# Attention and two MoE layers on one core: the second MoE's weight decoding, first pass on another engine

## Chip, cores, metric

One core of one Trainium2 chip runs the whole kernel in one launch. The metric is the device time of one execution in microseconds (us). The engines are PE (matrix products), DVE (vector), ACT (activations), POOL (GpSimd) and SP, which only issues DMAs here.

## What is computed

Attention with a learned bias on relative positions, then two MoE-like layers, on 4 x 576 tokens:

```python
scores = q @ k.T / sqrt(64) + bias(pos)          # 4 batches, 8 heads, 576 x 576
x  = softmax(scores) @ v                         # x: 2304 x 512
h  = x @ w_in;  s = h * softmax(h)               # first MoE, 1024 wide
x  = layernorm(s) * g_ln @ w_out                 # 2304 x 512
y  = (sigmoid(x @ w_gate) * (x @ w_val)) @ w_out2   # second MoE, 1536 wide
```

The weights of both MoEs arrive as 64-bit floats. [...]

## The kernel before

**Products.** PE multiplies 16-bit floats. Every 32-bit matrix is split in a high and a low half, and three products (high x high, high x low, low x high) take the place of one. The first MoE works tile by tile (18 tiles of 128 tokens): product with `w_in` (L789), exponential and sums (L810 to L819, on ACT and DVE), the layernorm's factor and its scaling on POOL (L822, L823), transposes on PE (L832) with the split of the result by ACT and DVE (L834, L835), product with `w_out` (L846), and the result `x2` stored to DRAM. The variance that L822 needs is L820 on DVE.

**Decoding of a weight.** `decode` (L185) works on a loaded block whose 32-bit words alternate low, high. First pass, L191: the high word, read as a 32-bit float, times 2 to the power -112, into the target `w`. Low pass, L192: the upper 16 bits of the low word, scaled, as an integer, in place. Then two bit passes on DVE: L193 shifts `w` left by 3 and ors the low part in, L195 ors the sign in. L191 and L192 run on ACT. L191 reads the high words with a step of two words and writes without a gap.

**The second MoE's weights.** 18 "pairs" of 1 MB, each 128 x 1024 elements, go through `w2_dec` (L1156): gate and value weights for three column blocks jc = 0, 1, 2 (pairs 0 to 11), then the output weights (12 to 17). After a pair's decoding ACT sums its squares (L1169). When a block of gate or value is complete, its scale is made (`w2_scale_gate`, `w2_scale_val`), and `w2_split` splits it: L720 on POOL scales 128 x 512 into `w2tmp`, ACT takes the high half (L721), POOL or, for every second piece, DVE the low half (L722). For the output weights ACT does the scaling and POOL the twelve low halves.

**Loads.** `load_pair` (L1084 and on) issues each pair as two DMAs on SP's queue. Pairs 1, 2, 5 and 6 land in buffers named `gv`, all others in two buffers named `wraw` (pair 0 in a third) that take turns, so that from pair 9 on a load starts when the pair two before has been decoded.

**Uses.** The gate and value products of the second MoE's first group of tokens, j = 0 to 11, are the matmuls of L1404 into `s_ps`, 24 to a j; four of them use one column block. The text calls j = 0 "group one", j = 4 "group five" and so on. Two banks take turns; ACT's sigmoid (L1409) and DVE's product (L1410) empty them. Then come the products with the output weights (L1436) and, for the other tokens, seven products in place of eight (L1368).

**Order.** A scheduler inside the framework orders the instructions of ACT, DVE, POOL, SP and, here, PE by its own estimate of when each could run and by priorities. Each engine then runs its own list strictly in order. So a change of one instruction can move others.

Of the kernel before, what the change touches and what calls it, by code (L numbers as in the profile page):

```python
# [13 lines left out]
ACTF = mybir.ActivationFunctionType  # L14
ALU = mybir.AluOpType
# [87 lines left out]
def attn_moe_kernel(  # L103
# [7 lines left out]
    act, dve, pool, pe, sp = nc.scalar, nc.vector, nc.gpsimd, nc.tensor, nc.sync  # L111
# [70 lines left out]
    def flat(a):  # L182
        return a.rearrange("b h s d -> (b h s d)").rearrange("(p f) -> p f", p=128)

    def decode(w, raw, engine):  # L185


        wi = w.bitcast(I32)
        hw = raw[:, :, 1].bitcast(F32)
        low = raw[:, :, 0]  # L190
        act.activation(out=w, in_=hw, func=ACTF.Copy, scale=2.0 ** -112)  # L191
        act.activation(out=low, in_=low.bitcast(U16)[:, :, 1], func=ACTF.Copy, scale=2.0 ** -13, bias=-0.4999)  # L192
        dve.scalar_tensor_tensor(out=wi, in0=wi, scalar=3, in1=low, op0=ALU.logical_shift_left, op1=ALU.bitwise_or)  # L193
        if engine is dve:
            dve.scalar_tensor_tensor(out=wi, in0=raw[:, :, 1], scalar=-0x80000000, in1=wi,  # L195
                                     op0=ALU.bitwise_and, op1=ALU.bitwise_or)
        else:
            act.activation(out=hw, in_=hw, func=ACTF.Sign)
            pool.tensor_tensor(out=w, in0=w, in1=hw, op=ALU.mult)
# [528 lines left out]
    def w1_steps():  # L728
        wst = sm0.tile([128, 2, 8], F32, name="wst")

        def dec(part, i):
            if part == 0:
                kk, n = divmod(i, 2)
                raw = load_w(wr_p, w_in, slice(128 * kk, 128 * kk + 128), slice(512 * n, 512 * n + 512))
            else:
                raw = load_w(wr_p, w_out, slice(128 * i, 128 * i + 128), slice(0, DM))
            w = wf[part][:, i]
            decode(w, raw, pool if i % 8 < W1P else dve)
            j = wd_p.tile([128, 512], F32, name="wjunk", tag="wsgn")
            act.activation(out=j, in_=w, func=ACTF.Square, scale=(gcol[:, i:i + 1] if part else 1.0),  # L740
                           accum_out=wst[:, part, i:i + 1])
# [160 lines left out]
    for n, (bb, hp) in enumerate(order):  # L902
        t0 = used[bb, hp]
        for nm, src, prep, lag in (("k", k, prep_k, 0), ("v", v, prep_v, LAG_PV)):
            if (bb, hp) == (0, 0):
                continue
            f = freed[order[n - 8]] + lag + 1 if n >= 8 else 4 * (n // 2 - 1) if n >= 4 else 0
# [171 lines left out]
    def load_pair(mat, jc, cc):  # L1079
        n = len(loads) // 2  # L1080
        if n in (1, 2, 5, 6):
            raw = ring("gv", [128, 2, 512, 2], I32)
        else:
            raw = w2r_p[n in (3, 7) or (n > 8 and n % 2)].tile([128, 2, 512, 2], I32, name="wraw", tag="wraw")  # L1084
        r0 = 256 * cc + (512 * jc if mat == 2 else 0)
        src = (w_gate, w_val, w_out2)[mat]
        cols = slice(0, DM) if mat == 2 else slice(512 * jc, 512 * jc + 512)
        for c in range(2):
            with tc.issue_after(loads[-1].ins):
                loads.append(sp.dma_start(out=raw[:, c].rearrange("p f t -> p (f t)"),  # L1090
                                          in_=src[r0 + 128 * c:r0 + 128 * c + 128, cols].bitcast(I32)))
        return raw
# [63 lines left out]
    def w2_dec(mat, jc, cc):  # L1156
        raw = w2raw.pop((mat, jc, cc), None)
        if raw is None:
            raw = load_pair(mat, jc, cc)
        w = w2f[mat][:, 4 * jc + 2 * cc:4 * jc + 2 * cc + 2].rearrange("p c f -> p (c f)")  # L1160
        decode(w, raw.rearrange("p c f t -> p (c f) t"), dve)
        if mat == 1:
            j = w2d_p.tile([128, 1024], BF16, name="w2sq", tag=f"w2sq{cc}")
            for c in range(2):
                w2h["sq", jc, 2 * cc + c] = j[:, 512 * c:512 * c + 512]
        else:
            j = w2t_p.tile([128, 1024], BF16, name="w2junk", tag="w2sgn")
        n = 6 * mat + 2 * jc + cc
        act.activation(out=j, in_=w, func=ACTF.Square, accum_out=w2st[:, n:n + 1])  # L1169
# [36 lines left out]
    def decs(m, jc):  # L1206
        return [(2, lambda cc=cc: w2_dec(m, jc, cc)) for cc in range(2)]
# [40 lines left out]
    first = [sum(sizes[:g]) for g in range(len(sizes))]  # L1248
# [307 lines left out]
```

## Time and profile before

| | |
|---|---|
| median of 3 runs | 1041.68 us (1038.64 to 1043.49) |
| the profiled execution | 1044.08 us, of which the span of its instructions 1042.3 us |
| PE busy | 898.6 us, 86% of the span |
| DVE busy | 725.1 us, 70% |
| ACT busy | 644.3 us, 62% |
| POOL busy | 390.4 us, 37% |

Attention fills the time up to about 550 us. Between 550 and 670 us three things overlap: the last four tiles of the first MoE, the decoding and splitting of all weights of the second, and its first gate products. After that PE works alone for the most part. All the passes that the change touches lie between 556 and 656 us. A share of busy time over the whole span tells little here; the stage must be read by itself, and in it which wait of PE ends last.

### The profile page before, as it was taken

Reading aid. Unit: us, or ns where it says so; the run is one execution under the profiler, and the core shown is the slowest. Engines: PE = TensorE matmul, PEld = TensorE weight load, DVE = VectorE, ACT = ScalarE, POOL = GpSimd, SP = SyncE. Lnnn points to the kernel's source line nnn. Section 1 sums busy time; section 2 is a strip of 40 time slices with the busy share of each in tenths; the row PEclk is TensorE's granted clock in tenths of the full one; section 3 lists DMA queues with packets and bytes.
Section 4 is the critical chain, followed back from the end, with each engine's and each line's share of the span. In section 5 each row is a group of like instructions: output and inputs, shape, how many; then the busy total and the mean of one; then the engine's idle time right before and its main releaser. Section 6 shows DMA issues by size and latency. Waiting matters only on the chain. (4 is left out here: it accounts for less than half of the span.)

```text
span 1042.3 us, 23926 instructions
## 1 busy us (share of the span) xinstructions
PE 898.6 (86%) x9620; PEld 634.8 (61%) x9620; DVE 725.1 (70%) x1487; ACT 644.3 (62%) x1275; POOL 390.4 (37%) x362
## 2 busy tenths in 40 slices
PE   2646665679888789999998989899999999999998
PEld 2634444455666556677775656346668847866873
DVE  6878899776577676667666987659936744771760
ACT  3788886757776888878876888674333322332320
POOL 3257656565666656655650486340000000000000
PEclk9666675769998999999998999899999999999999
DMA  7988999999999899899878444101020010000001
GB/s 222 282 255 205 247 254 246 219 206 189 189 191 198 174 207 179 176 219 207 160 137 310 172 158 171 58 1 61 22 61 1 1 61 21 1 11 31 2 1 41
DMA packets 257360, 144.57 MB, mean 139 GB/s; under 512 B 216417, under 2 KB 231777, under 8 KB 257249
## 3 DMA queue, kind: packets, MB, share of 16 engines
q1 hardware_dynamic: 253952, 139.90, 56.5%
q0 software_dynamic: 2048, 1.58, 0.6%
q8 instruction: 75, 1.23, 0.5%
q10 hardware_dynamic: 1248, 1.57, 0.4%
q14 instruction: 37, 0.30, 0.1%
HBM read 80.36 MB, written 20.19 MB: 96 GB/s over the span
## 5 line engine op out<-in xcount | busy, mean ns | idle before, releaser
L616 POOL TENSOR_TENSOR p<-p,p 128x1024 f16<-128x1024 f32 x72 | 158.0, 2194 | 123.3 <-ACT p L615 86.0
L1292 DVE TENSOR_TENSOR fr<-prod,fr 128x512 f32<-128x512 f32 x126 | 85.1, 688 | 92.3 <-PE prod L1368 90.6
L1436 PE MATMUL ops<-w2f,gv 128*128 128x512 f16 x648 | 142.5, 379 | 0.0
L604 ACT ACTIVATE p<-p,m,sc 128x576 f32<-128x576 f32 x144 | 123.9, 862 | 2.4
L597 DVE CUSTOM_DVE_ANT_0 p<-score,gk 128x576 f32<-128x576 f32 x144 | 102.9, 751 | 11.6 <-PE score L579 7.0
L846 PE MATMUL x2ps<-lt,w1f 128*128 128x128 f16 x1728 | 106.2, 221 | 3.5 <-ACT lt L834 1.9
L1436 PEld LDWEIGHTS <-gv 128*128 128x128 f16 x648 | 63.4, 98 | 73.7
L1404 PE MATMUL s_ps<-xb,w2f 128*128 128x512 f16 (+1 forms) x576 | 101.4, 335 | 3.7 <-DVE acc L162 3.4
L846 PEld LDWEIGHTS <-w1f 128*128 128x128 f16 x1728 | 101.0, 99 | 4.1 <-issue 1.6
L640 PE MATMUL xps<-gk,pt 128*128 128x64 f16 (+1 forms) x2240 | 86.8, 202 | 15.8 <-DMA pt<-p 14.1
L640 PEld LDWEIGHTS <-pt 128*128 128x128 f16 (+1 forms) x2240 | 81.9, 107 | 26.3 <-DMA pt<-p 17.0
L463 PEld LDWEIGHTS <-mask 128*128 128x128 f16 (+1 forms) x1312 | 62.2, 118 | 53.3 <-issue 23.4
L1368 PEld LDWEIGHTS <-w2f 128*128 128x128 f16 x864 | 84.5, 98 | 11.8 <-issue 1.1
L1404 PEld LDWEIGHTS <-w2f 128*128 128x128 f16 x576 | 56.9, 100 | 47.0 <-issue 7.4
L1273 ACT ACTIVATE gv<-fr 128x512 f16<-128x512 f32 (+1 forms) x60 | 34.8, 586 | 81.4 <-DVE fr L1426 70.5
L789 PE MATMUL hps<-w1f,xt 128*128 128x512 f16 x312 | 78.5, 398 | 5.5 <-DVE gk L262 2.6
L463 PE MATMUL bp<-rhs,mask 128*128 128x64 f16 (+1 forms) x960 | 50.0, 220 | 28.6 <-DVE gb L489 11.5
L574 PE MATMUL score<-gk,qt 64*128 64x512 f16 x384 | 59.8, 418 | 15.4 <-DVE m L597 7.0
L1368 PEld LDWEIGHTS <-w2s 128*128 128x128 f16 x648 | 63.4, 98 | 7.3
L789 PEld LDWEIGHTS <-xt 128*128 128x128 f16 x384 | 38.1, 102 | 48.8 <-issue 14.0
L615 ACT ACTIVATE p<-p 128x1152 f16<-128x1152 f32 x54 | 62.4, 1157 | 7.0 <-DMA pt<-p 4.9
L602 ACT ACTIVATE m<-m,sc 128x1 f32<-128x1 f32 x144 | 39.3, 286 | 32.9 <-DVE m L597 32.6
(207 smaller groups left out, 1760.7 us busy)
## 6 DMA issues: line engine op xcount, KB each, us to landing
gk<-bias_d SPq DMA_DIRECT2D x24, 576.0 KB
wraw<-in_moe_w_out_dram SPq DMA_DIRECT2D x20, 512.0 KB
sraw<-in_q_dram SPq DMA_DIRECT2D x12, 384.0 KB
sraw<-in_k_dram SPq DMA_DIRECT2D x12, 384.0 KB
sraw<-in_v_dram SPq DMA_DIRECT2D x12, 384.0 KB
bias_d<-gk SPq DMA_DIRECT2D x8, 576.0 KB
qraw<-in_q_dram SPq DMA_DIRECT2D x64, 64.0 KB
kv<-in_k_dram SPq DMA_DIRECT2D x32, 128.0 KB
```

The source lines that it names most:

```text
L463: pe.matmul(big[0:np_, jj // 8, o:o + 64], lhsT, rhs[i].rearrange("p c h g -> p (c h g)"), start=(i == 0), stop=(i == 1),)
L597: dve.tensor_tensor_reduce(out=pp[:, hh], in0=score[:, 960 * hh:960 * hh + S], in1=bi, scale=1.0, scalar=-3.0e38, op0=ALU.add, op1=ALU.max ...
L604: act.activation(out=pp[:, hh], in_=pp[:, hh], func=ACTF.Exp, bias=m[:, 2 + hh:3 + hh], scale=col(C), accum_out=sm[:, c + hh:c + hh + 1])
L615: act.activation(out=hi, in_=pp, func=ACTF.Copy)
L616: pool.tensor_tensor(out=p16[:, :, 640:1152], in0=view(pp, 0, [[640, 2], [1, 512]]), in1=view(p16, 0, [[1280, 2], [1, 512]]), op=ALU.subtract)
L640: pe.matmul(o, a, b_, start=(n == 0), stop=(n == len(seq) - 1))
L789: pe.matmul(h, xt[:, xl, kk, off:off + 128], win16[:, 2 * kk + n, wl], start=(kk == 0 and xl == 0 and wl == 0), stop=(kk == 3 and xl == 1),)
L846: pe.matmul(ps[:, dc], wout16[:, f, wl, 128 * dc:128 * dc + 128], lt[:, ll, f], start=(n == 0), stop=(n == 23))
L1292: dve.tensor_tensor(out=out_, in0=a, in1=b, op=op)
L1368: pe.matmul(p[:, jf, 0:nn], w(wl, kk, jf), x(xl, kk), start=(m == 0), stop=(m == 5))
L1404: pe.matmul(ps[:, 0:n], w[:, 4 * (j // 4) + c, wl, o:o + 128], xx[:, 0:n, c, xl, :], start=(m == 0), stop=(m == 11))
L1436: pe.matmul(ps, gvs[j // 4][:, gl, j % 4, 128 * tt:128 * tt + 128], w2h16[2][:, j, wl], start=(m == 0), stop=(m == 35))
```

## The change

The second MoE's `decode` gets POOL as the engine of its first pass. The first MoE's 16 blocks keep ACT.

```diff
--- before.py
+++ after.py
@@ -182,13 +182,16 @@
     def flat(a):
         return a.rearrange("b h s d -> (b h s d)").rearrange("(p f) -> p f", p=128)
 
-    def decode(w, raw, engine):
+    def decode(w, raw, engine, first=None):
 
 
         wi = w.bitcast(I32)
         hw = raw[:, :, 1].bitcast(F32)
         low = raw[:, :, 0]
-        act.activation(out=w, in_=hw, func=ACTF.Copy, scale=2.0 ** -112)
+        if first is None:
+            act.activation(out=w, in_=hw, func=ACTF.Copy, scale=2.0 ** -112)
+        else:
+            first.tensor_scalar(out=w, in0=hw, scalar1=2.0 ** -112, scalar2=None, op0=ALU.mult)
         act.activation(out=low, in_=low.bitcast(U16)[:, :, 1], func=ACTF.Copy, scale=2.0 ** -13, bias=-0.4999)
         dve.scalar_tensor_tensor(out=wi, in0=wi, scalar=3, in1=low, op0=ALU.logical_shift_left, op1=ALU.bitwise_or)
         if engine is dve:
@@ -1158,7 +1161,7 @@
         if raw is None:
             raw = load_pair(mat, jc, cc)
         w = w2f[mat][:, 4 * jc + 2 * cc:4 * jc + 2 * cc + 2].rearrange("p c f -> p (c f)")
-        decode(w, raw.rearrange("p c f t -> p (c f) t"), dve)
+        decode(w, raw.rearrange("p c f t -> p (c f) t"), dve, pool)
         if mat == 1:
             j = w2d_p.tile([128, 1024], BF16, name="w2sq", tag=f"w2sq{cc}")
             for c in range(2):
```

Three lines are added ahead, so L192 becomes L195, L193 becomes L196, L195 becomes L198, and every line behind them moves by three; the first pass on POOL is L194.

The scheduler orders the stage anew on every engine. In names below, `wraw_9413` is pair 0, `gv_9709` pair 1, `wraw_10694`, `wraw_10703` and `wraw_10712` are pairs 15, 16 and 17; `w2f0`, `w2f1`, `w2f2` are gate, value and output weights.

DVE at the start of the stage, before. `hs_9646` is the copy of tile 14's first product:

```order
L193 SCALAR_TENSOR_TENSOR w2f0_9694<-w2f0_9694,wraw_9413 128x1024
L707 TENSOR_TENSOR xt_8631<-xtp_9623,xt_8631 128x256
L195 SCALAR_TENSOR_TENSOR w2f0_9694<-wraw_9413,w2f0_9694 128x1024
L707 TENSOR_TENSOR xt_8632<-xtp_9623,xt_8632 128x256
L800 ISA hs_9646,mm_9645<-hps_9632,zero_79 128x512
L800 ISA mm_9645 128x1
L193 SCALAR_TENSOR_TENSOR w2f0_9694<-w2f0_9694,gv_9709 128x1024
L835 TENSOR_TENSOR lt_9759<-ltp_9760,lt_9759 128x512
L800 ISA hs_9646,mm_9645<-hps_9648,zero_79 128x512
```

DVE there now:

```order
L710 TENSOR_TENSOR xt_8632<-xtp_9623,xt_8632 128x256
L803 ISA hs_9646,mm_9645<-hps_9632,zero_79 128x512
L803 ISA mm_9645 128x1
L196 SCALAR_TENSOR_TENSOR w2f0_9694<-w2f0_9694,wraw_9413 128x1024
L838 TENSOR_TENSOR lt_9759<-ltp_9760,lt_9759 128x512
L198 SCALAR_TENSOR_TENSOR w2f0_9694<-wraw_9413,w2f0_9694 128x1024
L803 ISA hs_9646,mm_9645<-hps_9648,zero_79 128x512
L803 ISA mm_9645 128x1
L196 SCALAR_TENSOR_TENSOR w2f0_9694<-w2f0_9694,gv_9709 128x1024
```

The copy of tile 14's first half product stood behind pair 0's two bit passes and now stands ahead of both.

POOL late in the stage, before, from the third value split of block 1 (`w2tmp_10342`) on:

```order
L720 TENSOR_SCALAR w2tmp_10342<-w2f1_9695,sw_81 128x512
L722 TENSOR_TENSOR w2f1_9695<-w2tmp_10342,w2f1_9695 128x512
L720 TENSOR_SCALAR w2tmp_10346<-w2f1_9695,sw_81 128x512
L720 TENSOR_SCALAR w2tmp_10553<-w2f0_9694,sw_81 128x512
L720 TENSOR_SCALAR w2tmp_10557<-w2f0_9694,sw_81 128x512
L722 TENSOR_TENSOR w2f0_9694<-w2tmp_10553,w2f0_9694 128x512
L720 TENSOR_SCALAR w2tmp_10561<-w2f0_9694,sw_81 128x512
L720 TENSOR_SCALAR w2tmp_10681<-w2f0_9694,sw_81 128x512
L722 TENSOR_TENSOR w2f0_9694<-w2tmp_10561,w2f0_9694 128x512
```

POOL there now, from pair 15's first pass on:

```order
L194 TENSOR_SCALAR w2f2_9696<-wraw_10694 128x1024
L723 TENSOR_SCALAR w2tmp_10342<-w2f1_9695,sw_81 128x512
L723 TENSOR_SCALAR w2tmp_10346<-w2f1_9695,sw_81 128x512
L725 TENSOR_TENSOR w2f1_9695<-w2tmp_10342,w2f1_9695 128x512
L194 TENSOR_SCALAR w2f2_9696<-wraw_10703 128x1024
L723 TENSOR_SCALAR w2tmp_10553<-w2f0_9694,sw_81 128x512
L723 TENSOR_SCALAR w2tmp_10557<-w2f0_9694,sw_81 128x512
L194 TENSOR_SCALAR w2f2_9696<-wraw_10712 128x1024
L725 TENSOR_TENSOR w2f0_9694<-w2tmp_10553,w2f0_9694 128x512
L723 TENSOR_SCALAR w2tmp_10561<-w2f0_9694,sw_81 128x512
```

The same splits now have the first passes of pairs 15, 16 and 17 among them, and each of these waits for a load.

ACT late in the stage, before, from pair 17's first pass on; `fr_10996` is the sigmoid of group five:

```order
L191 ACTIVATE w2f2_9696<-wraw_10712 128x1024
L192 ACTIVATE wraw_10712<-wraw_10712 128x1024
L854 DMA x2_d_58<-x2_10677 128x1024
L1169 ACTIVATE w2junk_10710,w2st_9697<-w2f2_9696 128x1024
L1273 ACTIVATE gv_10764<-fr_10927 128x512
L1409 ACTIVATE fr_10965<-s_ps_10940,sw_81 128x512
L1169 ACTIVATE w2junk_10719,w2st_9697<-w2f2_9696 128x1024
L1409 ACTIVATE fr_10996<-s_ps_10971,sw_81 128x512
```

ACT there now, from pair 16's low pass on:

```order
L195 ACTIVATE wraw_10703<-wraw_10703 128x1024
L1172 ACTIVATE w2junk_10531,w2st_9697<-w2f2_9696 128x1024
L1172 ACTIVATE w2junk_10540,w2st_9697<-w2f2_9696 128x1024
L724 ACTIVATE w2f0_9694<-w2tmp_10553 128x512
L195 ACTIVATE wraw_10712<-wraw_10712 128x1024
L724 ACTIVATE w2f0_9694<-w2tmp_10557 128x512
L1412 ACTIVATE fr_10996<-s_ps_10971,sw_81 128x512
L1412 ACTIVATE fr_11026<-s_ps_11001,sw_81 128x512
```

The first pass is gone; the sigmoid of group five stands a few places behind pair 17's low pass, as it did, and now that low pass itself waits for the load.

## Rows read from the trace of the kernel before

**Rows 1.** Busy us (instructions) of PE, PEld, DVE, ACT, POOL; then clock, DMA.
```profile
556.00:656.50 100.50, 86.07 (x740) 56.63 (x740) 84.36 (x152) 85.16 (x126) 54.16 (x40) 0.91 0.57 199
680.00:780.00 100.00, 99.28 (x603) 58.77 (x602) 75.11 (x133) 47.00 (x85) 10.44 (x9) 1.00 0.10 34
```

**Rows 2.** Timeline of PE: start us, us, instruction [idle before, what ended it].
```profile
590.81 0.24 PE L846 MATMUL x2ps<-lt,w1f 128*128 128x128 f16 x1 [1.90 <-ACT lt L834]
593.86 3.05 PE L846 MATMUL x2ps<-lt,w1f 128*128 128x128 f16 x48
603.64 4.44 PE L789 MATMUL s_ps<-w1f,xt 128*128 128x512 f16 x12 [2.31 <-DVE mm L800]
626.53 0.38 PE L1179 MATMUL tot<-w2st,ones_sb 128*128 128x1 f32 x2 [3.01 <-ACT w2junk L1169]
656.52 1.03 PE L1404 MATMUL s_ps<-xb,w2f 128*128 128x512 f16 x2 [3.43 <-DVE acc L162]
```

**Rows 3.** Line L191 (duration ns min/median/max, first and last start); and a wait.
```profile
L191 ACT ACTIVATE w2f<-wraw x14: 1106/1138/1157, 556.2 to 656.0; 128x1024 f32<-128x1024 f32 x14
L191 ACT ACTIVATE w2f<-gv x4: 1135/1176/1182, 560.0 to 583.5; 128x1024 f32<-128x1024 f32 x4
DVE w2f L193 <- ACT wraw L192: 7.2, 8, 1.7
```

**Rows 4.** Lines of POOL, ns min/median/max; then groups in 556 to 671 us.
```profile
L823 POOL TENSOR_SCALAR e<-e,mm x18: 1189/1197/3256, 264.5 to 624.5; 128x1024 f32<-128x1024 f32 x18
L720 POOL TENSOR_SCALAR w2tmp<-w2f,sw x24: 687/854/2294, 581.3 to 668.9; 128x512 f32<-128x512 f32 x24
L199 POOL TENSOR_TENSOR w1f<-w1f,wraw x8: 1284/1298/1568, 79.1 to 150.5; 128x512 f32<-128x512 f32 x8
L720 POOL TENSOR_SCALAR w2tmp<-w2f,sw 128x512 f32<-128x512 f32 x24 | 28.3, 1185 | 22.5 <-ACT w2junk L1169 14.2 <-DVE mm L811 6.8 <-DVE w2f L722 0.8
L722 POOL TENSOR_TENSOR w2f<-w2tmp,w2f 128x512 f16<-128x512 f32 x12 | 19.8, 1648 | 8.3 <-ACT w2f L721 8.1
```

**Rows 5.** Timeline of POOL and DVE where the two meet.
```profile
580.12 1.20 POOL L823 TENSOR_SCALAR e<-e,mm 128x1024 f32<-128x1024 f32 x1
580.59 1.79 DVE L193 SCALAR_TENSOR_TENSOR w2f<-w2f,gv 128x1024 int32<-128x1024 int32 x1 [0.85 <-ACT gv L192]
588.20 1.22 DVE L195 SCALAR_TENSOR_TENSOR w2f<-gv,w2f 128x1024 int32<-128x1024 int32 x1
588.31 2.12 POOL L722 TENSOR_TENSOR w2f<-w2tmp,w2f 128x512 f16<-128x512 f32 x1 [0.75 <-ACT w2f L721]
```

**Rows 6.** Timeline of DVE at the start of the stage.
```profile
559.59 1.22 DVE L195 SCALAR_TENSOR_TENSOR w2f<-wraw,w2f 128x1024 int32<-128x1024 int32 x1
564.27 0.69 DVE L800 CUSTOM_DVE_ANT_0 hs<-hps,zero 128x512 f32<-128x512 f32 x1 [3.13 <-PE hps L789]
578.26 0.15 DVE L820 TENSOR_SCALAR mm<-mm 128x1 f32<-128x1 f32 x1
```

**Rows 7.** Timeline of POOL: scalings of the last tiles.
```profile
611.64 1.19 POOL L823 TENSOR_SCALAR e<-e,mm 128x1024 f32<-128x1024 f32 x1
624.53 3.26 POOL L823 TENSOR_SCALAR e<-e,mm 128x1024 f32<-128x1024 f32 x1
```

**Rows 8.** Timeline of DVE and ACT: ends of decoded pairs, and a load's landing.
```profile
607.60 1.21 DVE L195 SCALAR_TENSOR_TENSOR w2f<-wraw,w2f 128x1024 int32<-128x1024 int32 x1
640.66 1.46 DVE L195 SCALAR_TENSOR_TENSOR w2f<-wraw,w2f 128x1024 int32<-128x1024 int32 x1
647.92 1.21 DVE L195 SCALAR_TENSOR_TENSOR w2f<-wraw,w2f 128x1024 int32<-128x1024 int32 x1
647.03 1.15 ACT L191 ACTIVATE w2f<-wraw 128x1024 f32<-128x1024 f32 x1 [0.82 <-DMA wraw<-in_moe_w_out_dram]
```

**Rows 9.** Timeline of POOL, the last split before 672; chain, groups five to eight.
```profile
670.01 1.16 POOL L722 TENSOR_TENSOR w2f<-w2tmp,w2f 128x512 f16<-128x512 f32 x1
669.05 11.46 PE s_ps L1404 x53
```

## The prediction

> **What bounds the kernel now.** I read the busy time by stage first. From 680 us on PE is busy 99.28 of 100 us, and the page's slices show it so up to the end; in the stage before, 556 to 656.5 us, it is busy 86.07 of 100.5 us while ACT (85.16) and DVE (84.36) are nearly full and POOL has 54.16 [rows 1]. The change touches that stage alone. PE's work in it is fixed, so the end of the kernel moves by as much as PE's arrival at the gate products moves. Second view: PE's own timeline, for what ended its idle time. It waits 1.90 us at 590.81 (ACT's high half of a transposed tile), 2.31 at 603.64 (DVE's copy of a product), 3.01 at 626.53 (ACT's sum of squares) and 3.43 at 656.52, where the fifth gate group begins [rows 2]. The last is named after a later DVE step; the group really waits for a bank that ACT and DVE empty late. These four, 10.7 us, are what a relief of ACT could give back.
>
> **What is removed.** ACT loses the 18 passes of L191 (14 at 1.138 and 4 at 1.176 us, medians), 20.6 us of 85 [rows 3]. None is on PE's path by itself. What they delay is the pass on the low words behind them: DVE waited 7.2 us for it in eight places [rows 3].
>
> **What is added.** POOL gets 18 passes of 1024 elements with one input. The trace has no such pass with a step of two words. The nearest row is L823, one input, 1024 elements, two operations, step one: 1.19 us when nothing blocks it [rows 4]. From below, nothing suggests less than about 1.1. From above: L199 reads one operand with the step and takes 1.284 for 512 elements, where the plain L722 takes 1.16 [rows 4, 9], so twice that difference on top, 1.44. I take 1.2, as the row with the same operand count: 21.6 us on POOL.
>
> **The port.** DVE's 1024-element pass with two SBUF inputs takes 1.22 us alone (L195 at 588.20). POOL's L722 that began 0.11 us behind it took 2.12 in place of 1.16: it ended 1.01 us after DVE did. The other way round, DVE's L193 that began under POOL's L823 took 1.79 and ended 1.06 us after that [rows 5]. So the two exclude each other, each holding the port for about 1.05 us of its 1.2.
> [...]
> The ledger from 556 to 671: DVE has 36 bit passes (37.8 us held at 1.05), 4 of L813 (4.4) and 17 short ones of 0.55 (9.4); POOL has 24 of L720 at 0.56 (13.4; 0.687 alone), 12 of L722 at 1.02 (12.2) [rows 4], 5 of L823 (5.3) and 5 of L822 at 0.43 (2.2). That is 84.7 of 115 us. The new passes add 18 x 1.05 = 18.9, making 103.6, or 90%. It fits, with 11 us of slack where there were 30. Neither end of the pass's price (1.1 to 1.44, held for 0.15 less) breaks it: 101.8 to 107.9.
>
> **The new order, step by step.** Tile 14 to 17 are the last four tiles of the first MoE; "pair" is a load of 1 MB of weights.
> 1. Entry. DVE ran the two bit passes of pair 0, the second at 559.59, while it would have waited 3.13 us for PE's product at 564.27 [rows 6]. Now that product's copy stands ahead of them, so 2.4 us of DVE work move into a stretch in which DVE does not rest. Tile 14's variance, at 578.26 before [rows 6], comes at 580.7.
> 2. First transposed tile. PE's product of tile 14, at 593.86 [rows 2], needs DVE's low half of it. Until then POOL gets three passes more (pairs 6 to 8), 3.2 us of the port; DVE's three waits for low words there (0.85, 0.27, 0.72, within the 7.2 of [rows 3]) go. So 593.9 + 2.4 + 3.2 - 1.8 = 597.7, and at worst 600 where none of the three waits was on the way; PE stands still for it.
> 3. Tiles 15 and 16. Their two scalings now stand side by side on POOL. Tile 16's was done at 611.64 + 1.19 = 612.8 [rows 7]. DVE reaches its variance 5 to 7 us after step 2's half tile (two bit passes, one of L813 and the short ones), and two scalings of 1.2 and a blocked pass follow: 607 to 610. PE has made up step 2 and leads by 2 to 3 us; its wait of 2.31 is gone.
> 4. Tile 17. Its scaling took 3.26 us from 624.53, blocked by DVE [rows 7]; I get 624.5 to 625.5 for its end in place of 627.8. The sum-of-squares matmul that cost 3.01 us now stands after the last tile. PE ends the fourth gate group 2.7 us ahead.
> 5. Group five. The 3.43 us go if the splits that it needs are done. They were done long before; now they stand on POOL behind first passes that wait for loads. Two buffers take turns, and a load starts when DVE is through with the pair two before. Before, from pair 9 to pair 15 that took (649.1 - 608.8)/3 = 13.4 us a turn [rows 8], of which the load is 4.9 (issued when the pass at 640.66 ended, landed at 647.03 [rows 8]). Step 1 to 3 put pairs 7 and 8 some 10 us behind, and POOL's splits stay at 657 to 659: group five ends near 660 where it ended near 662.
> 6. Group seven. On ACT the sigmoid of group five stands behind pair 17's low pass. By step 5 pair 15's load lands at about 652, pair 17's a turn of 10.4 to 13.4 later: 662.4 to 665.4, and group seven starts at 666 to 668.6. Before it started at 669.05 + 5 x 0.216 = 670.1 (53 matmuls in 11.46 us [rows 9]). PE leads by 1.5 to 4.6; I take 3.
> 7. Group nine needs the last gate and value splits, done at 671.2 before [rows 9] against a need at 681.6. Now at about 679, against a need at 677 to 680: nought to 2 lost. The output weights' scale follows within PE's two groups of 10.4 us, which hide it; without them it would cost 6.
> Sum: -3 us, from -4.6 to +2. Against the profiled run's 1044.08 that is 1041.1; the median of the runs, 1041.68, lies 2.4 lower, so 1038.7, rounded to **1039**.
>
> **Rivals.**
> A. ACT was the bound and the port has room. Then the four waits of [rows 2] go without the new one of step 2, and group five runs at PE's full rate: -10.7, 1031, from 1027 to 1036. For it: ACT's 85%, and the port's 11 us of slack. Against it: DVE is as full as ACT, and POOL's queue stands in order behind loads. Chance 0.28.
> B. The port becomes the bound, with the splits as its place. L720 took 1.185 us on average with 0.687 alone, a factor of 1.72 [rows 4]. If the first passes suffer the same, they take 2.06 each and push the bit passes as far; the decode turn grows by four times 0.86 from 13.4 to about 17, three turns lie between pair 11 and pair 17, so pair 17's load comes 11 us later than in step 6 and PE has lost 8 by group seven: 1050, from 1046 to 1056. It decides from a turn of 14.5 us on. Chance 0.23.
> C. The pass does not cost what one-input passes cost, but as two-input ones do: twice L722's 1.16 for 512 elements [rows 9], 2.3 us. Then 18 more us on the port make 122 of 115, and the end moves by these 7 and most of B's 8: 1055. Against it: L823. Chance 0.07.
> That the change does nothing would need POOL to skip the pass; the new order shows 18 of them.
>
> **How the numbers follow.** My forecast (1036.5 to 1046.5) has 0.42, A 0.28, B 0.23, C 0.07. A measurement of this kernel can tell about 0.5%, 5.2 us, from no change. So faster by more: 0.28; within: 0.42; slower: 0.30, with the upper part of the forecast's own range counted as within. The range runs from 1029 (A's tail left out, 0.07) to 1052 (C and the top of B left out, 0.12).
>
> **What would show it.** Right: in the profile after, 18 POOL passes of about 1.2 to 1.6 us on average; ACT near 66 us in 556 to 656; DVE's pair 0 after 564; PE's wait before tile 14's product 6 us or more; its wait of 3.0 gone; a wait of some 4 us before group seven that ACT ends. Wrong: passes above 2 us (B, C), no wait at tile 14 (A), or PE waiting at group nine for POOL's splits by more than 3 us, which would put step 7 at fault. If the load, not the queue, sets the decode turn, the turn stays at 13.4 and the forecast holds whatever the passes cost.

## The result, and the profile after

The changed kernel takes 1055.9 us (median of 4 runs, 1050.9 to 1058.9) against 1042.6 in the same session: a ratio of 1.0121, interval 1.008 to 1.0163. It is slower, by some 12.6 us by that ratio (the two medians lie 13.3 us apart), where 1039 was forecast with a range up to 1052. The execution that the trace shows is the fastest of the four, 1050.9 us with a span of 1049.1.

Executions reach this stage up to some 3 us earlier or later whatever the kernel (554.2 to 560.4 us in the traces here), so I measure the stage from the transposes of the last attention output to the first product of the later token groups. PE's timeline (start us, us, instruction, idle before and what ended it), first before, then after:

```profile
557.68 1.12 PE L689 MATMUL xtp<-id_sb,xn 128*128 128x128 f32 x4 [3.35 <-DVE xn L676]
780.06 1.47 PE L1368 MATMUL prod<-xb,w2f 128*128 128x256 f16 x12 [0.78 <-ACT ob L1440]
```
```profile
554.24 1.12 PE L692 MATMUL xtp<-id_sb,xn 128*128 128x128 f32 x4 [3.18 <-DVE xn L679]
588.73 1.97 PE L835 MATMUL ltp<-id_sb,e 128*128 128x128 f32 x8 [4.83 <-POOL e L826]
644.80 0.28 PE L1182 MATMUL tot<-w2st,ones_sb 128*128 128x1 f32 x2
667.58 15.87 PE L1407 MATMUL s_ps<-xb,w2f 128*128 128x512 f16 x60 [6.06 <-DVE fr L1413]
710.82 4.40 PE L1407 MATMUL s_ps<-xb,w2f 128*128 128x256 f16 x24 [2.42 <-DVE fr L1413]
717.55 2.78 PE L1407 MATMUL s_ps<-xb,w2f 128*128 128x256 f16 x24 [1.91 <-DVE fr L1413]
786.84 1.47 PE L1371 MATMUL prod<-xb,w2f 128*128 128x256 f16 x12 [0.78 <-ACT ob L1443]
```

The stage grew from 222.4 to 232.6 us, and what lies behind the first product is 262.2 us in both. Read from one trace, such a length is good to some 3 us: e2_forms below, whose engines run this stage in the order of before, has 219.4. PE's waits behind those transposes tell more: they add up to 13.5 us before (15.0 in e2_forms) and 23.5 after. (Line numbers from L191 on stand three higher.) The waits are others than in [rows 2]: the one of 3.01 us before the sums of squares is gone (644.80), and new ones are for tile 14's scaling on POOL, at group seven, and at 711 and 718 us, where PE hardly rested before.

Busy us by stage, as in [rows 1]:

```profile
556.00:656.50 100.50, 89.06 (x763) 58.75 (x765) 82.44 (x138) 62.29 (x95) 90.54 (x47) 0.94 0.54 185
680.00:780.00 100.00, 95.68 (x579) 57.41 (x578) 87.07 (x147) 50.84 (x95) 20.20 (x17) 0.98 0.07 25
```

ACT fell from 85.16 to 62.29, as planned. POOL rose by 36 us in that stretch, where 21.6 were priced for all passes, and from 680 us on PE now loses 3.6 us more than before, a stretch that the prediction had called full. The pass itself, which answers [rows 3], by its line (ns min/median/max, first and last start), and its first one on POOL's timeline, behind a scaling of the same size:

```profile
L194 POOL TENSOR_SCALAR w2f<-wraw x14: 2817/2864/3945, 554.5 to 665.3; 128x1024 f32<-128x1024 f32 x14
L194 POOL TENSOR_SCALAR w2f<-gv x4: 2826/3362/3838, 557.3 to 581.5; 128x1024 f32<-128x1024 f32 x4
```
```profile
553.29 1.20 POOL L826 TENSOR_SCALAR e<-e,mm 128x1024 f32<-128x1024 f32 x1
554.46 2.84 POOL L194 TENSOR_SCALAR w2f<-wraw 128x1024 f32<-128x1024 f32 x1
```

The splits' scaling that shares POOL's queue, 0.854 us in the median in [rows 4], is now at 1.040:

```profile
L723 POOL TENSOR_SCALAR w2tmp<-w2f,sw x24: 682/1040/2183, 579.2 to 683.0; 128x512 f32<-128x512 f32 x24
```

The scaling of a tile takes 1.20 us, the pass 2.84, with no DVE operation with two SBUF inputs beside it. The 18 of them come to some 57 us where 21.6 were priced.

### The profile page after: what moved, and what is told of

Read it like the earlier page. It is cut to its first block, busy times and chain, and to the rows that moved or that the text cites. A ratio compares the mean times of both kernels' runs of the same rounds, so it can differ in the third digit from the quotient of the medians.

```text
span 1049.1 us, 23952 instructions
## 1 busy us (share of the span) xinstructions
PE 899.9 (86%) x9617; PEld 636.6 (61%) x9620; DVE 738.9 (70%) x1487; ACT 626.8 (60%) x1257; POOL 450.0 (43%) x380
## 5 line engine op out<-in xcount | busy, mean ns | idle before, releaser
L1407 PE MATMUL s_ps<-xb,w2f 128*128 128x512 f16 (+1 forms) x576 | 102.9, 337 | 12.3 <-DVE fr L1413 10.6
L792 PE MATMUL hps<-w1f,xt 128*128 128x512 f16 x312 | 76.1, 389 | 5.1 <-DVE gk L265 2.4
```

Of the source, the lines that this page charges most:

```text
L792: pe.matmul(h, xt[:, xl, kk, off:off + 128], win16[:, 2 * kk + n, wl], start=(kk == 0 and xl == 0 and wl == 0), stop=(kk == 3 and xl == 1),)
L1407: pe.matmul(ps[:, 0:n], w[:, 4 * (j // 4) + c, wl, o:o + 128], xx[:, 0:n, c, xl, :], start=(m == 0), stop=(m == 11))
```

## The experiments

Ratios are to the kernel before in the same session, with 95% intervals; 1% is 10.4 us.

### What the pass costs, and why

**e2_forms** adds eleven POOL operations, each twice, behind the last tile of the kernel before.

> The kernel before, with eleven POOL operations added twice behind its last tile, where DVE is nearly idle, on scratch data (the second and third group of weights are no longer needed there): the price of each form undisturbed. Theory 1 (one operation costs): forms with one operation take 2.8 us per 1024 elements with either step, forms with two 1.2. Theory 2 (the step of two words costs): all forms with the step take 2.8, all with step one 1.2. A mixture (only one operation together with the step, or only an immediate number in place of a column) would show as just those rows at 2.8.

Their lines (ns min/median/max). In order: one operation with a step of two words, two operations with that step, one operation with step one, two with step one, and the last two again with 512 elements and a scale by column where there are two operations:

```profile
L1495 POOL TENSOR_SCALAR w2f<-w2f x2: 2860/3016/3172, 962.9 to 982.8; 128x1024 f32<-128x1024 f32 x2
L1496 POOL TENSOR_SCALAR w2f<-w2f x2: 1397/1397/1397, 965.8 to 986.0; 128x1024 f32<-128x1024 f32 x2
L1498 POOL TENSOR_SCALAR w2f<-w2f x2: 3087/3088/3089, 969.4 to 989.7; 128x1024 f32<-128x1024 f32 x2
L1499 POOL TENSOR_SCALAR w2f<-w2f x2: 1044/1049/1054, 972.6 to 992.8; 128x1024 f32<-128x1024 f32 x2
L1502 POOL TENSOR_SCALAR w2f<-w2f x2: 1487/1488/1489, 976.2 to 996.5; 128x512 f32<-128x512 f32 x2
L1503 POOL TENSOR_SCALAR w2f<-w2f,sw x2: 692/692/693, 977.8 to 998.1; 128x512 f32<-128x512 f32 x2
```

Theory 1 holds. The form with one operation costs two to three times the form with two, at either step (3.02 against 1.40 us, and 3.09 against 1.05), as it does for 512 elements (1.49 against 0.69 us). DVE was not as idle there as the expectation has it. The 0.35 us between 1.40 and 1.05 are no price of the step: both times that operation began while DVE ran one with two SBUF inputs, and it ended 1.0 us after it, as in [rows 5]. The first time, on the timelines of DVE and POOL (the DVE row holds two operations, the second from 965.50 to 966.19):

```profile
964.90 1.28 DVE L1426 SCALAR_TENSOR_TENSOR fr<-fr 128x512 f32<-128x512 f32 x2
965.81 1.40 POOL L1496 TENSOR_SCALAR w2f<-w2f 128x1024 f32<-128x1024 f32 x1
```

In the kernel of the next run the same form with the step takes 1.10 us at least, so the step adds some 0.05 us. A scale by column together with the step took 2.04 us, also between such DVE operations; its undisturbed price is open. The kernel before has no POOL scaling of the form with one operation: all write two, and in all but the tile scaling (L823) the second does nothing.

**e1_two_ops** gives the pass that second operation.

```diff
-first.tensor_scalar(out=w, in0=hw, scalar1=2.0 ** -112, scalar2=None, op0=ALU.mult)
+first.tensor_scalar(out=w, in0=hw, scalar1=2.0 ** -112, scalar2=0.0, op0=ALU.mult, op1=ALU.add)
```

> The changed kernel, with the pass on the high words written with a second operation that does nothing (multiply, then add 0), as the scaling of the splits and the other cheap POOL rows of the trace have it; the read with a step of two words stays. In the changed kernel the pass took 2.82 us undisturbed where 1.2 was priced. Theory 1 (the form with one operation is what costs): the pass falls to 1.2 to 1.5 us undisturbed, the shared port has room again, and the kernel lands where the forecast's sum had it, 1036 to 1046. Theory 2 (the step of two words is what costs): the pass stays at 2.7 to 2.9 and the kernel at 1051 to 1059. Theory 3 (the price is not the cause; POOL's splits wait in order behind passes that wait for loads): whatever the price, 1050 to 1058.

The pass fell to 1.13 us in the median (1.10 at least), and the kernel stayed at 1055.9, 1.0134 (1.0099 to 1.0169). So theory 1 was right on the price and wrong on the time, which is that of theory 3. But the scheduler had made another order for this program on all engines, so price and order had both changed. They had to be parted: the same cheap pass costs 0.65 and 0.67% less in the two orders of the next table, so this third order is worth another 7 us.

### Price and order apart

The next four kernels carry a table of one kernel's instruction order, and chain each engine's instructions by it (shortened):

```diff
+for d_ in table:
+    at_ += d_
+    i_ = traced[at_]
+    if i_.engine in last_:
+        tc.add_manual_dep(i_, last_[i_.engine].name, NoSync)   # order of issue alone, no wait
+    last_[i_.engine] = i_
```

> The pass on POOL as in the changed kernel, with its one operation, but every engine's instructions kept in the order of the kernel before; the pass stands on POOL where it stood in that kernel's overall order on ACT. Only the engine of the pass and its price differ from the kernel before. Theory P (the pass's price is the loss: 18 times 2.8 us on a port that had 30 us of slack): 1048 to 1058. Theory O (the new order is the loss, price and port matter little): 1036 to 1044.

> The order of the kernel before on every engine, and the pass on POOL with two operations (1.33 us measured in place of 3.1). Theory P: what the forecast's sum was made for, no change or better, 1034 to 1044. Theory O: the same, 1034 to 1044, and equal to the kernel with one operation in this order.

> The order of the changed kernel on every engine, but the pass on ACT as in the kernel before, at its place in the changed kernel's overall order. Nothing is added to POOL or to the port. Theory P: the loss is gone, 1038 to 1046. Theory O: it stays, 1050 to 1058.

> The order of the changed kernel on every engine, the pass on POOL with two operations. Against the changed kernel only the price of the pass differs, 1.33 in place of 3.1 us. Theory P: most of the loss is gone, 1036 to 1046. Theory O: it stays, 1050 to 1058.

| | pass on ACT | on POOL, two operations | on POOL, one operation |
|---|---|---|---|
| order of before | 1 | 1.0069 (1.0049 to 1.0090) | 1.0178 (1.0149 to 1.0206) |
| order of the changed kernel | 1.0069 (1.0041 to 1.0098) | 1.0067 (1.0042 to 1.0093) | 1.0121 (1.0080 to 1.0163) |

Neither theory holds alone; the dearest kernel, 1062.9 us, lies above the range of both. Along the lower row the changed kernel's 12.6 us are 7.2 for the new order with the pass still on ACT, nothing for the move in its cheap form, and 5.6 for the form, of which the two intervals leave anything from nothing to 1.2%. Along the upper row the move costs 7.2 in its cheap form, against both theories, and the form 11.3 more, which is clear of noise. The shares depend on the path. The order alone is a loss, so is the move alone, and the two together lose no more than either.

### What the move costs at its cheap price

Two kernels part the move into what it takes and what it gives, both in the order of before. **e10_relief_alone** leaves the 18 passes out, **e11_load_alone** keeps them on ACT and adds 17 idle ones on POOL (edits shortened, against the kernel before).

```diff
-act.activation(out=w, in_=hw, func=ACTF.Copy, scale=2.0 ** -112)                  # e10
-dve.scalar_tensor_tensor(out=wi, in0=wi, scalar=3, in1=low, op0=ALU.logical_shift_left, ...)
+dve.scalar_tensor_tensor(out=wi, in0=raw[:, :, 1], scalar=0x3FFFFFFF, in1=low, op0=ALU.bitwise_and, ...)
```
```diff
 act.activation(out=w, in_=hw, func=ACTF.Copy, scale=2.0 ** -112)                  # e11
+pool.tensor_scalar(out=spare, in0=hw, scalar1=2.0 ** -112, scalar2=0.0, op0=ALU.mult, op1=ALU.add)
```

> The kernel before in its own order on every engine, with the 18 passes on the high words left out: DVE's first bit pass reads the high word of the raw weight itself (and masks it in place of shifting it), so the weights come out wrong, but each other instruction and each order stands as it was. It shows what relieving ACT of its 20.6 us is worth when nothing is put on POOL. If ACT was the bound (rival A): 1030 to 1036. If DVE is the bound beside it: 1037 to 1043, and the change had little to win at any price.

> The kernel before in its own order, ACT's passes kept, and beside each of 17 of them a POOL operation of the same shape (two operations, 1.33 us), whose result nobody reads: it writes a part of the last weights that is decoded later. It shows what the load on POOL and the port costs by itself; no decoding step waits for it. Port theory (each meeting of a POOL operation with a DVE operation with two SBUF inputs makes one of them longer, and DVE has no slack for it): 1048 to 1056, DVE's such operations some 8 us longer in all. Chain theory (the pass now stands behind POOL's other work, so that decoding starts later): 1040 to 1045, since nothing waits for these.

The relief gives 0.9975 (0.9959 to 0.9992), 2.6 us. The load costs 1.0102 (1.0084 to 1.0120), 10.6. Together 8.0, where the whole move in this order measured 7.2. The chain theory falls: nothing waits for these operations, and they cost as much as the pass itself.

**e17_memset_load** puts an operation in their place that only writes.

```diff
-pool.tensor_scalar(out=spare, in0=hw, scalar1=2.0 ** -112, scalar2=0.0, op0=ALU.mult, op1=ALU.add)
+pool.memset(spare, 0.0)
```

> The kernel with 17 idle POOL operations beside ACT's passes, with each of them turned into one that only writes: the same 128x1024 elements set to zero, at the same place in POOL's queue. It was 1051.5 with the operation that reads and writes (1.11 to 1.13 us each undisturbed). If it is POOL's queue that costs (splits and the last scaling stand behind these operations): 1047 to 1052, for about as long an operation. If it is the meetings with DVE, it depends on whether the writing alone takes the port: DVE's operations longer and 1047 to 1052, or not longer and 1041 to 1045.

It takes 0.95 us on POOL every time, at the same places of the queue, and the kernel 1.0018 (0.9997 to 1.0038): the loss is gone, or at most 0.4%. Groups of DVE's first bit pass in 556 to 671 us (busy us, mean ns, idle before and what ended it), of before, of e11 and of e17:

```profile
L193 DVE SCALAR_TENSOR_TENSOR w2f<-w2f,wraw 128x1024 int32<-128x1024 int32 x14 | 18.6, 1332 | 7.3 <-ACT wraw L192 7.2
```
```profile
L196 DVE SCALAR_TENSOR_TENSOR w2f<-w2f,wraw 128x1024 int32<-128x1024 int32 x14 | 21.9, 1568 | 4.7 <-ACT wraw L195 4.7
```
```profile
L196 DVE SCALAR_TENSOR_TENSOR w2f<-w2f,wraw 128x1024 int32<-128x1024 int32 x14 | 18.7, 1333 | 7.4 <-ACT wraw L195 7.3
```

With the reading load these 14 passes take 3.3 us more and the waits shrink by 2.6; with the writing one both stand as before. All 36 bit passes of DVE take 47.9 us before, 55.4 with the reading load and 48.9 with the writing one, and POOL's last five tile scalings 8.0, 10.5 and 8.0. One meeting of each kind, on the timelines of POOL and DVE, e11 and then e17:

```profile
587.49 1.67 POOL L193 TENSOR_SCALAR w2f<-wraw 128x1024 f32<-128x1024 f32 x1
588.15 2.09 DVE L198 SCALAR_TENSOR_TENSOR w2f<-gv,w2f 128x1024 int32<-128x1024 int32 x1
```
```profile
583.31 0.95 POOL L193 MEMSET w2f<- 128x1024 f32 x1
583.27 1.22 DVE L198 SCALAR_TENSOR_TENSOR w2f<-gv,w2f 128x1024 int32<-128x1024 int32 x1
```

Below, both run at once and neither is longer than alone (0.95 and 1.22 us). Above, both are: 1.67 us where the least in e11 is 1.11, and 2.09 in place of 1.22. So the price of the load is these meetings, and a longer queue on POOL by itself cost nothing that could be measured (1.0018). The traces show that the two hold each other up, not where: "the port" is the prediction's name for it. Two differences stay between e11 and e17. The operation that reads also holds the raw buffer, but each ended 2.6 us or more before DVE was through with that buffer, so the next load never waited for it. And it waits for its own load, which the one that only writes does not: in e11 POOL stood 13.8 us for loads. The chain of work that ended last in e11 has no load on it between 555 and 672 us, so these waits did not set the time there. In the changed kernel that chain has three:

```profile
603.25 7.38 DMA wraw<-in_moe_w_val_dram
619.62 5.00 DMA wraw<-in_moe_w_out_dram
644.28 5.83 DMA wraw<-in_moe_w_out_dram
```

No run parts what these cost from the price of the pass.

### What relieves the port

**e4_scale_on_act** and **e12_old_order_scale_on_act** move the scaling of the 24 gate and value splits from POOL to ACT, in the changed kernel and in the cheap form in the old order; **e13_two_ops_scale_on_act** is the cheap form with the order that it gets by itself. **e5_every_second** leaves every other pass on ACT.

```diff
-act if mat == 2 else None, dve if mat < 2 and c % 2 else None)     # e4, e12, e13: in w2_split
+act, dve if mat < 2 and c % 2 else None)
-decode(w, raw.rearrange("p c f t -> p (c f) t"), dve, pool)        # e5
+decode(w, raw.rearrange("p c f t -> p (c f) t"), dve, pool if cc else None)
```

> The changed kernel, with the scaling of the 24 gate and value splits by ACT in place of POOL. It takes 24 times 0.69 us from POOL and the port and gives ACT some 24 times 0.65, which brings ACT back from 62 to about 78 of the 100.5 us. If the full port is what the change lost its time to (99% of 556 to 671 us in the changed kernel), this gives back 13 us of port: 1043 to 1049. If instead the passes' place in POOL's queue is what costs, the low halves of the splits still stand behind them: 1049 to 1056.

> The changed kernel, with only the second pass of each two on POOL (nine of 18), the others on ACT as before. Price and port theory: 9 passes of 2.7 us put 24 us on the port beside the 84.7 of the kernel before, 109 of 115: it just fits, and ACT is 10 us lighter: 1038 to 1045. Queue theory: half the passes still stand ahead of the splits and wait for their loads: about half the loss, 1046 to 1050.

> The order of the kernel before, the pass on POOL with two operations, and the scaling of the 24 gate and value splits moved from POOL to ACT, at its place in the overall order. POOL loses 24 times 0.69 us and gains 18 times 1.33. Port theory: the meetings fall back, DVE's operations are at most some 4 us longer than before, and of the 8 us that the pass cost in this order most are gone: 1041 to 1047. Otherwise, with ACT again near 80 of 100.5 us, nothing is gained against the same order without this move: 1048 to 1053.

> The changed kernel with the two-operation pass and the scaling on ACT, in the order that this program gets by itself. With the one-operation pass it took 1045.2. Each pass is 1.7 us shorter on POOL: 1036 to 1043 where the port decides; a new order may take that away, as it did with the two-operation pass alone (1055.9 in its own order, 1049.9 in the changed kernel's).

e4: 1.0026 (1.0008 to 1.0045). e5: 1.0036 (1.0016 to 1.0056). e12: 1.0023 (1.0003 to 1.0044), against 1.0069 without the scaling moved and in the same order. e13: 1.0018 (1.0000 to 1.0036). All four take most of the loss away; none is faster than the kernel before. Only e12 changes nothing else. The others have orders of their own, which take part: e4's 18 passes still come to 55 us on POOL, more than e7's 24, and it loses less. With ACT's relief worth some 2.6 us there was little to win.

### What the new order costs

In e8 the pass is on ACT and only the order is new. PE's waits in the stage add up to 20.7 us where they were 13.5, and two of them, where PE hardly rested before, hold 5.2:

```profile
711.22 2.78 PE L1407 MATMUL s_ps<-xb,w2f 128*128 128x256 f16 x24 [1.69 <-DVE fr L1413]
717.96 4.45 PE L1407 MATMUL s_ps<-xb,w2f 128*128 128x256 f16 x24 [3.52 <-DVE fr L1413]
```

They are the waits of the changed kernel at 710.82 and 717.55. Who keeps DVE from the product stands on its timeline, first before, then after:

```profile
695.02 1.89 DVE L1292 TENSOR_TENSOR fs<-w2f 128x512 f32<-128x512 f16 x3
...
699.42 0.68 DVE L1410 SCALAR_TENSOR_TENSOR fr<-s_ps,fr 128x512 f32<-128x512 f32 x1
```
```profile
696.22 4.79 DVE L1295 TENSOR_TENSOR fs<-w2f 128x512 f32<-128x512 f16 x3
...
702.98 1.65 DVE L1295 TENSOR_TENSOR w2s<-fs,w2s 128x512 f16<-128x512 f32 x1
704.55 1.64 DVE L1295 TENSOR_TENSOR fs<-fs,w2f 128x512 f32<-128x512 f32 x1
...
710.09 0.68 DVE L1413 SCALAR_TENSOR_TENSOR fr<-s_ps,fr 128x512 f32<-128x512 f32 x1
```

These are the sums of the decoded weights for the later token groups. Before, 7 of them run between two products; after, 13 (the expectation below counts 11), for 13.9 us, and some take more than twice their 0.69 us while POOL is still splitting the last weights beside them, as here beside the two at 702.98 and 704.55 (1.65 and 1.64 us):

```profile
702.87 2.77 POOL L725 TENSOR_TENSOR w2f<-w2tmp,w2f 128x512 f16<-128x512 f32 x2 [2.41 <-ACT w2f L724]
```

**e14_sums_later** starts them two gate groups later in the changed kernel.

```diff
-            if (g, j) == (0, 9):
+            if (g, j) == (0, 11):
                 glob["so"] = low_
```

> The changed kernel, with DVE's sums of the gate and value weights for the later token groups started two gate groups later. Up to 690 us the order is that of the changed kernel. In its trace 11 of these sums ran ahead of the product of a gate group at 710.09, and PE waited 2.42 us at 710.82 and 1.91 at 717.55. Theory (this is a part of what the new order costs, and no step of the prediction looked past 680 us): both waits go, 4.3 us, 1050 to 1054. Rival (PE's waits come from late weights, which the sums only fill): the waits stay or move, 1054 to 1059.

1.0046 (1.0025 to 1.0067) in place of 1.0121, and the stage is full again:

```profile
680.00:780.00 100.00, 100.00 (x609) 59.44 (x607) 78.79 (x147) 56.42 (x102) 19.58 (x19) 1.00 0.06 22
```

So this queue is a large part of the loss: 0.75%, 7.8 us, of which the two intervals leave 0.1 to 1.4%. The kernel came to 1048.4, below the 1050 to 1054 expected from its two waits of 4.3 us. The traces show what can go beside the waits: from group seven to the first product of the later groups PE's same products take 119.3 us in the changed kernel and 113.1 in e14. Of these 6.2 us 4.3 are the two waits; the other 1.9 are products at a lower granted clock, 0.89 of full speed in 706 to 722 us.

Whether an order alone can also win, three runs show. **e15_half_scaling_on_act** moves 12 of the scalings to ACT in the kernel before, **e16_half_scaling_old_order** does so in the order of before, and **e18_before_in_e15_order** moves nothing and takes over the order of e15.

```diff
-act if mat == 2 else None, dve if mat < 2 and c % 2 else None)     # e15, e16
+act if mat == 2 or c % 2 else None, dve if mat < 2 and c % 2 else None)
```

> The kernel before, its passes on ACT, with the scaling of those 12 gate and value splits whose low half DVE makes also on ACT in place of POOL, in the order the program gets by itself. If 22 us more on POOL and the port cost 10 us, 8 us less should give back 2 to 4 where ACT has room for 8 us more: 1036 to 1040. If ACT, at 85 of 100.5 us, is as full, or a new order costs: 1041 to 1050.

> The same in the order of the kernel before on every engine, so that no new order takes part: 1036 to 1040 if relieving the port pays, 1041 to 1045 if ACT's 8 us weigh as much.

> The kernel before, nothing moved between engines, but every engine's instructions in the order that e15_half_scaling_on_act got (that kernel took 1036.7 where before took 1043.0; the same edit in the order of before took 1044.8). If the gain was the order alone: 1033 to 1039, the same as there. If it needs both, the order and the 12 scalings off POOL: 1040 to 1046.

e15: 0.9947 (0.9925 to 0.9969). e16: 1.0020 (0.9999 to 1.0040). e18: 0.9925 (0.9903 to 0.9946), 1035.5 us, the fastest of all. The gain is the order alone; the scaling moved gives nothing. So with every instruction on its engine, the order is worth 7.8 us to one side (e18) and 7.2 to the other (e8). Which places in e15's order bring it was not tried.

## Why the prediction was wrong

**What is added: 1.2 us for the pass.** The first step to fail: 2.82 undisturbed. L823 was called nearest for its one input, and the text says that it has two operations, but took the input count as what matters. It is the operation count (e2: 3.09 us with one, 1.05 with two, both at step one). With two operations the price was right (1.10 to 1.14 undisturbed). The upper bound, 1.44, was drawn from the step, which adds some 0.05 here, and not from the form, of which the trace had no row: a bound that holds only for the feature that it varies. Rival C had nearly the time, 1055, by a wrong reason (the form with one operation is dearer than two inputs, 1.49 us for 512 elements in e2 against L722's 1.16, and plain reads are as dear as those with a step, 3.09 against 3.02 us for 1024). It costs 5.6 us in the new order and 11.3 in the old.

**The port: 11 us of slack left.** The second, worth 7.2 us in the old order beside 11.3 for the form, and nothing in the new one. At the cheap price the ledger was right in its sum, some 19 us added, and wrong in what it concluded: that a sum below the stretch's length means room. Added time met DVE's bit passes where they overlapped, and a meeting made DVE or POOL later by up to a microsecond (2.12 us in place of 1.16 on POOL in [rows 5], 2.09 in place of 1.22 on DVE in e11). e11: 17 operations of 1.13 us, 19 us of port, DVE's bit passes 7.5 us longer, 10.6 us at the end. DVE had no more rest than ACT (84.36 of 100.5); the text used that in step 1 and against rival A, and not against the ledger's slack.

**What is removed, and rival A.** The four waits of 10.7 us were taken as ACT's to give back. All 20.6 us of relief, with nothing in return, give 2.6 (e10). The text's doubt, that DVE is as full, was the right one; its chance of 0.28 for A was too high.

**The new order.** Steps 1 to 6 hold as places. DVE's pair 0 began at 559.99, behind the product at 559.37; tile 14's variance came 23.0 us behind the transposes where it was 20.6, and 2.4 had been worked out. PE stood before tile 14 (4.83 us, 6 or more expected), the wait of 3.01 is gone, and group seven waited as in step 6: ACT's sigmoid at 665.88 stands behind pair 17's low pass at 664.26. But it waited 6.06 us, not 4. (The sum's lower end of 4.6 is a slip: from 670.1 to 666 it is 4.1.) A turn of the decoding took 13.8 us over pairs 9 to 15, where it was 13.4 [rows 8]. Over pairs 11 to 17, which rival B names, it took 14.9, just above B's mark of 14.5, and 1055.9 lies in B's range. But B's 8 us lost by group seven did not come: it began 113.3 us behind the transposes, where it was 112.5. A lead of 3 had been forecast there.

**Step 7, and what was not looked at.** The sum ended near 680 us, on the strength of PE being 99.28 of 100 us busy there [rows 1]. It was so busy because of DVE's order in that stretch, and the change moved that order too. The two waits at 711 and 718 are in no step. In the two traces 9.4 of the stage's 10.2 us lie behind the start of group seven: 4.3 in these waits, and 5.1 as the same products at a lower granted clock. Before, a stretch with a granted clock of 0.54 of full speed lay ahead of group seven, behind the wait of 3.43 us. After, it lies behind group seven's wait of 6.06 (0.50), and a smaller loss comes with the two later waits (0.89). One stretch before, then two after, in the columns of [rows 1]:

```profile
656.50:663.00 6.50, 6.48 (x17) 2.39 (x18) 4.28 (x6) 4.90 (x8) 1.27 (x2) 0.54 0.04 13
```
```profile
667.58:671.00 3.42, 3.42 (x9) 1.22 (x9) 3.32 (x4) 1.20 (x2) 3.42 (x3) 0.50 0.01 2
706.00:722.00 16.00, 11.68 (x71) 7.55 (x69) 16.00 (x23) 7.17 (x13) 4.31 (x3) 0.89 0.19 67
```

The clock only moved the loss between the parts of the stage; over the whole of it PE's products took 208.8 us before and 209.2 after, and the loss is its waits. The new order as a whole costs 7.2 us (e8), and no term of the sum stood for it.

The signs that the text had named as wrong were there: passes above 2 us, and of its right ones ACT's 62.29 and the moved waits. So the result lies above the range by two terms that it did not hold: a form without a row, and an order priced only where it was looked at.

## What to carry to other kernels

Price an operation from a row of the very same form, counting its operations as well as its inputs and elements; where there is none, say so and bound it from the dearest neighbour in each feature, not in one.

Room on average in what two engines share was not free here: DVE had little rest (84.36 of 100.5 us busy), and about half of what was added was lost in one order (10.6 us for 19), while in another the whole move cost nothing (1.0067 against 1.0069); so measure it in the order that will run, and look first for an operation that does not read (17 that only write: 1.0018).

Where a scheduler makes a new order for every edit, part edit and order before judging either: freeze the order, change the engine; then freeze the engines, change the order. Here the order alone moved the same work from 0.7% slower to 0.75% faster, as much to either side as the move did at its cheap price. Of the 7.2 us lost 5.2 lay in two waits some 40 us behind the last instruction that the edit touched.

## What the runs showed of the hardware

GpSimd's scaling by a number, for 1024 elements per partition read with a step of two words, took 2.82 us undisturbed with one operation (the changed kernel) and 1.10 with two, the second doing nothing (e1). With step one the form with two took 1.05 (e2). That is 2.75 ns an element for the form with one operation at the step of two words, and 1.02 for the form with two at step one.

An operation of GpSimd that only writes SBUF ran beside DVE's operations with two SBUF inputs without making either longer (e17): 17 of 17 took 0.94 to 0.95 us, those at 583.31 and 587.25 beside bit passes of 1.22 us, and DVE's 36 bit passes took 48.9 us in all where they took 47.9 without.
